# Two products interleaved from the first batch on, x of batch 0 by a casting DMA, and heads paired as neighbours

## The chip, the cores and the metric

One core of one Trainium2 chip. The metric is the device time of one execution in microseconds. A program's executions fall into a fast and a slow state; each run lists its granted TensorE clock. Profiles are of one execution, whose span is some 1.8 us shorter than its time.

## The reference, cut to what matters

```python
# x: (8, 8, 512, 64) batches, heads, rows, depth; state: (8, 8, 32, 64)
scores = scale * np.matmul(x, state.transpose(0, 1, 3, 2))   # softmax over the 32 states -> a
xread = np.matmul(a, state)
scores2 = scale * np.matmul(state, x.transpose(0, 1, 3, 2))  # softmax over the 512 rows -> a2
sread = np.matmul(a2, x)
attn = np.concatenate([xread, sread], axis=2)
# heads side by side: 4352 tokens of 512
h = tokens @ w_in                     # w_in 512 x 2048
out = gelu_exact(h) @ w_out           # w_out 2048 x 512
```

For each batch the kernel folds the state into the first weight (P = state times w_in, per head), so that the first product of a batch is P against the transposed attention weights a. The products: 256 matmuls of 128x512 for the first, 512 for the second, all batches together.

## The kernel before, cut to the parts concerned

Names as in the profile: `xb` is x of a batch as loaded (bf16), `x` the same rearranged by head pairs, `xT` its transpose, `pt` scores, `e` their exponentials, `a` normalised, `AT` its transpose, `p_ps`/`P` the folded weight, `hp`/`g` the first product and its Gelu, `op`/`osb` the second product and its eviction, `st_f`/`st_bf` states in fp32 and bf16. `pool` buffers with `space=PSUM` lie in the memory that TensorE writes to. Of the functions, `rearr` makes `x` of a batch, `xtr_dma` and `atr_dma` issue the transposing DMAs of `x` and of `a`, `scores`, `norm`, `pmat` and `sread` make `pt` and `e`, `a`, `P`, and the read of the state; a step of the first product is 2 matmuls and a Gelu (`M` in the changed kernel), a step of the second is 4 matmuls (`U`).

```python
ps_f = ctx.enter_context(tc.tile_pool(name="ps_f", bufs=6, space=bass.MemoryType.PSUM))
ps_o = ctx.enter_context(tc.tile_pool(name="ps_o", bufs=2, space=bass.MemoryType.PSUM))
...
st_rows = state.rearrange("b (t c) n d -> (c n) b t d", t=2)      # heads c and c+4 are a pair
nc.scalar.dma_start(out=st_f, in_=st_rows[:, 0, :, :])            # states of batch 0
...                                                               # x of batch 0: four fp32 DMAs, cast on VectorE
load_w_in(0)
load_w_in(1)
nc.gpsimd.dma_start(                                              # states of batches 1 to 7: ONE casting DMA
    out=st_bf[:, 1:B, :, :].rearrange("q b t d -> q (b t) d"),
    in_=st_rows[:, 1:B, :, :].rearrange("q b t d -> q (b t) d"),
)
load_x(1)
...
def steady(b):                       # what stands ahead of which first-product step of batch b
    nb = b + 1
    d[0] = [begin(nb), rearr(nb), load_x(b + 3), xtr_dma(nb)]     # lambdas left out
    d[4] = [scores(nb, 0), scores(nb, 1), norm(nb, 0), norm(nb, 1)]
    d[7] = [pmat(nb, (0, 1), act=((0, 1), (1, 1)))]
    d[8] = [atr_dma(nb)]
    d[12] = [sread(nb)]
    d[13] = [pmat(nb, (2, 3), act=((2, 1), (3, 1)))]
    d[14] = [srt(nb)]
...
lag = 16                             # the second product is 16 steps behind the first
mm1(b, s)                            # 2 matmuls and a Gelu
if done > lag:
    mm2(u)                           # 4 matmuls; two accumulators in turn
```

The softmax here doesn't subtract the row's maximum and nothing guards it: scores larger than these inputs give would overflow.

Of the kernel before, what the change touches and what calls it, by code (L numbers as in the profile page):

```python
# [17 lines left out]
def kernel(  # L18
# [25 lines left out]
    ps_f = ctx.enter_context(tc.tile_pool(name="ps_f", bufs=6, space=bass.MemoryType.PSUM))  # L44
    ps_o = ctx.enter_context(tc.tile_pool(name="ps_o", bufs=2, space=bass.MemoryType.PSUM))
# [11 lines left out]
    st_f = persist.tile([128, 2, D], FP32, name="st_f")  # L57
    st_bf = persist.tile([128, B, 2, D], BF16, name="st_bf")
    x0f = persist.tile([128, 2, HC, SJ * D], FP32, name="x0f")
    warm = persist.tile([128, 512], BF16, name="warm")  # L60
    ones = persist.tile([128, 1], BF16, name="ones")
# [3 lines left out]
    st_rows = state.rearrange("b (t c) n d -> (c n) b t d", t=2)  # L65
    x0_rows = x[0].rearrange("(t c) (p j) d -> p t c (j d)", t=2, j=SJ)
    nc.scalar.dma_start(out=st_f, in_=st_rows[:, 0, :, :])
    for c in range(HC):
        eng = nc.sync if c % 2 == 0 else nc.scalar
        eng.dma_start(out=x0f[:, :, c, :], in_=x0_rows[:, :, c, :])  # L70

    make_identity(nc, ident)
    nc.vector.memset(warm, 0.0)  # L73
    nc.gpsimd.memset(sbd, 0.0)
    nc.gpsimd.memset(ones, 1.0)

    def load_w_in(f):
        for t in range(2):
            nc.gpsimd.dma_start(  # L79
                out=w_in_bf[64 * t:64 * t + 64, :, f * 512:(f + 1) * 512],  # L80
                in_=moe_w_in[256 * t:256 * t + 256, f * 512:(f + 1) * 512].rearrange(
                    "(c d) f -> d c f", c=HC
                ),
            )
# [6 lines left out]
    xbs = {}  # L91

    def load_x(b):
        xb = xin.tile([128, H, SJ * D], BF16, name="xb", tag="xb")
        nc.gpsimd.dma_start(out=xb, in_=x[b].rearrange("h (p j) d -> p h (j d)", j=SJ))
        xbs[b] = xb

    load_w_in(0)
    load_w_in(1)
    nc.gpsimd.dma_start(  # L100
        out=st_bf[:, 1:B, :, :].rearrange("q b t d -> q (b t) d"),
        in_=st_rows[:, 1:B, :, :].rearrange("q b t d -> q (b t) d"),
    )
    load_x(1)
    load_w_in(2)
    load_w_in(3)
    load_w_out(0)
    load_w_out(1)
    load_x(2)
    load_w_out(2)  # L110
    load_w_out(3)
    load_x(3)


# [6 lines left out]
    def state_prep(b0, b1):  # L121
        n = b1 - b0
        if b0 == 0:
            nc.vector.tensor_copy(out=st_bf[:, 0, :, :], in_=st_f)
# [28 lines left out]
    def rearr(b):  # L153
        A = atts[b]
        eng = nc.vector if b < 3 else nc.gpsimd
        for t in range(2):
            eng.tensor_copy(  # L157
                out=A.x4[:, :, :, 64 * t:64 + 64 * t].rearrange("p j c d -> p c j d"),
                in_=xbs[b][:, 4 * t:4 * t + 4, :].rearrange("p c (j d) -> p c j d", d=D),
            )  # L160

    def rearr0(c):
        A = atts[0]
        nc.vector.tensor_copy(
            out=A.x4[:, :, c, :].rearrange("p j (t d) -> p t j d", t=2),
            in_=x0f[:, :, c, :].rearrange("p t (j d) -> p t j d", d=D),
        )

    def xtr0(c):
        A = atts[0]  # L170
        ps = ps_f.tile([128, SJ, 128], BF16, name="xT_ps", tag="f")
        for j in range(SJ):
            nc.tensor.transpose(ps[:, j, :], A.x4[:, j, c, :], ident)
        nc.scalar.copy(out=A.xT[:, :, c, :], in_=ps)

    def xtr(b, half):
        A = atts[b]
        ps = ps_f.tile([128, 2, SJ, 128], BF16, name="xT_ps", tag="f")
        for ci in range(2):
            for j in range(SJ):  # L180
                nc.tensor.transpose(ps[:, ci, j, :], A.x4[:, j, 2 * half + ci, :], ident)
        nc.vector.tensor_copy(out=A.xT[:, :, 2 * half:2 * half + 2, :].rearrange("p j c n -> p c j n"), in_=ps)

    def score_mms(b, c):
        A = atts[b]
        if c % 2 == 0:
            A.pt = ps_f.tile([128, SJ, 2, 2, NS], FP32, name="pt", tag="f")
        for j in range(SJ):
            nc.tensor.matmul(  # L189
                A.pt[:, j, :, c % 2, :],  # L190
                lhsT=A.xT[:, j, c, :],
                rhs=sbd[:, b, c, :],
                start=True,
                stop=True,
            )

    def expo(b, half):
        A = atts[b]
        nc.scalar.activation(  # L199
            out=A.e[:, :, 64 * half:64 * half + 64],  # L200
            in_=A.pt.rearrange("p j t c n -> p (j t) (c n)"),
            func=AF.Exp,
            scale=scale,
        )

    def xtr_dma(b):
        A = atts[b]
        nc.sync.dma_start_transpose(
            out=A.xT.rearrange("p j c n -> p (j c) n"), in_=A.x4.rearrange("p j c n -> p (j c n)")
        )  # L210

    def scores(b, half):
        score_mms(b, 2 * half)
        score_mms(b, 2 * half + 1)
        expo(b, half)
# [45 lines left out]
    def sread(b):  # L261
        A = atts[b]
        sr = ps_f.tile([128, 130], FP32, name="sr", tag="f")
        for o, n in ((0, D), (128, 1)):
            for t in range(2):
                for j in range(SJ):
                    for c in range(HC):
# [4 lines left out]
                            rhs=A.x4[:, j, c, 64 * t:64 * t + 64] if n == D else ones,  # L272
# [23 lines left out]
    def pmat(b, fs, act=()):  # L296
# [3 lines left out]
        for f in fs:  # L300
            ps = [ps_f.tile([128, 512], FP32, name="p_ps", tag="f") for t in range(2)]
# [10 lines left out]
        for f, ps in zip(fs, pss):  # L312
            for t in range(2):
                dst = Ps[b][:, t, f * 512:(f + 1) * 512]
                if (f, t) in act:
                    nc.scalar.copy(out=dst, in_=ps[t])  # L316
                else:
                    nc.vector.tensor_copy(out=dst, in_=ps[t])  # L318
# [33 lines left out]
    def mm2(u):  # L352
        b, r = u // 16, u % 16
        if b == 0:
            j, q = 2 * (r // 8) + r % 2, (r % 8) // 2
        else:
            j, q = r // 4, r % 4
        if q == 0:
            ops[j % 2] = ps_o.tile([128, d_model], FP32, name="op", tag="op")
        ps = ops[j % 2]  # L360
# [8 lines left out]
        if q == 3:  # L369
            rows = out[b * SB:b * SB + S, :].rearrange("(p j) n -> j p n", j=SJ)[j]  # L370
            evac(ps, [(rows, slice(0, 128))], last=(u == 16 * B - 1))
# [13 lines left out]
    def mm2_sr(s):  # L385
        ps = ps_o.tile([128, d_model], FP32, name="ops", tag="op")
# [14 lines left out]

    begin(0)
    keep_warm(6)
    state_prep(0, 1)
    for c in range(HC):
        rearr0(c)
    xtr0(0)
    xtr0(1)
    score_mms(0, 0)
    xtr0(2)  # L410
    score_mms(0, 1)
    expo(0, 0)
    xtr0(3)
    score_mms(0, 2)
    keep_warm(2)
    score_mms(0, 3)
    expo(0, 1)
    norm(0, 0)
    norm(0, 1)
    keep_warm(6)  # L420
    pmat(0, (0,), act=((0, 0), (0, 1)))
    keep_warm(4)
    atr(0)
    keep_warm(2)

    extra = {
        0: {
            1: [lambda: pmat(0, (1,))],
            3: [lambda: state_prep(1, B)],
            5: [lambda: begin(1), lambda: rearr(1), lambda: xtr(1, 0)],  # L430
            6: [lambda: xtr(1, 1), lambda: scores(1, 0), lambda: scores(1, 1)],
            7: [lambda: pmat(0, (2,))],
            8: [lambda: norm(1, 0), lambda: norm(1, 1)],
            10: [lambda: pmat(0, (3,))],
            12: [lambda: pmat(1, (0,))],
            13: [lambda: atr(1)],
            14: [lambda: pmat(1, (1,))],
        },
        1: {
            1: [lambda: sread(0), lambda: pmat(1, (2,))],  # L440
            2: [lambda: srt(0)],
            3: [lambda: pmat(1, (3,)), lambda: begin(2), lambda: rearr(2), lambda: xtr_dma(2)],
            4: [lambda: load_x(4), lambda: sread(1)],
            6: [lambda: srt(1)],
            8: [lambda: scores(2, 0), lambda: scores(2, 1), lambda: norm(2, 0), lambda: norm(2, 1)],
            10: [lambda: pmat(2, (0, 1), act=((0, 1), (1, 1)))],
            11: [lambda: atr_dma(2)],
            13: [lambda: sread(2)],
            14: [lambda: pmat(2, (2, 3), act=((2, 1), (3, 1)))],
            15: [lambda: srt(2)],  # L450
        },
    }

    def steady(b):
        nb = b + 1
        d = {}
        if nb >= B:
            return d
        d[0] = [lambda: begin(nb), lambda: rearr(nb)]
        if b + 3 < B:  # L460
            d[0].append(lambda: load_x(b + 3))
        d[0].append(lambda: xtr_dma(nb))
        d[4] = [
            lambda: scores(nb, 0),
            lambda: scores(nb, 1),
            lambda: norm(nb, 0),
            lambda: norm(nb, 1),
        ]
        d[7] = [lambda: pmat(nb, (0, 1), act=((0, 1), (1, 1)))]
        d[8] = [lambda: atr_dma(nb)]  # L470
        d[12] = [lambda: sread(nb)]
        d[13] = [lambda: pmat(nb, (2, 3), act=((2, 1), (3, 1)))]
        d[14] = [lambda: srt(nb)]
        return d

    u = 0
    lag = 16
    done = 0
    for b in range(B):
# [49 lines left out]
```

## Time and profile before

| | before |
|---|---|
| time, median of 3 | 236.54 us (236.05 to 237.08) |
| span of the profiled run | 234.7 us |
| TensorE busy | 217.1 us, 92% |
| granted clock | full from 12.2 us on |
| first matmul of the first product | 14.59 us |
| first matmul of the second product | 31.45 us |
| TensorE's largest wait | 5.4 us in six pieces, scores for the transposing DMA of x |

The views also show full clock before 12.2 us, but there the trace has no record of the clock: until then 128x512 matmuls last 0.61 to 0.63 us, and 0.38 us after, so the clock was at half.

Read the table from the last row up. TensorE sets the time; the waits and the start are all that a change of order can win.

### The profile page before, as it was taken

What the parts mean: (1) busy time and instruction counts of PE and PEld (TensorE: products, weight loads), DVE (VectorE), ACT (ScalarE), POOL (GpSimd) and SP (SyncE); (2) the same over time, 40 slices, a digit from 0 to 9 for tenths busy, and PEclk for the clock granted to TensorE, in tenths of its full rate; (3) what the DMA queues carried; (4) which work ended last, traced back from release to release, by engine and by line L of the source; (5) the groups of instructions that cost most, each with busy time, mean ns of one, the idle gap of its engine ahead of it and who ended that gap; (6) DMA issues with size and microseconds to landing.
All of it is one profiled execution on the core that took longest, in us unless ns stands there. A gap on an engine that the chain in (4) does not pass through costs nothing.

```text
span 234.7 us, 4315 instructions
## 1 busy us (share of the span) xinstructions
PE 217.1 (92%) x1844; PEld 100.7 (43%) x1844; DVE 85.3 (36%) x162; ACT 124.7 (53%) x208; POOL 28.1 (12%) x38
## 2 busy tenths in 40 slices
PE   5996799889979999999799999999999999999993
PEld 1543244434334444444344444444444444567441
DVE  2655974274135413631181317231623111111120
ACT  2577754485467446744494549454955454426000
POOL 8745001304000400030002000000000000000000
PEclk9999999999999999999999999999999999999999
DMA  7999999972923294252804061316131111211122
GB/s 205 149 178 206 202 205 185 126 161 26 226 76 86 56 165 98 62 75 53 128 0 106 31 143 38 89 47 134 46 92 45 47 45 55 80 46 47 27 65 87
DMA packets 38707, 23.12 MB, mean 98 GB/s; under 512 B 21920, under 2 KB 34464, under 8 KB 38688
## 3 DMA queue, kind: packets, MB, share of 16 engines
q0 software_dynamic: 13376, 8.09, 25.3%
q1 hardware_dynamic: 24352, 14.03, 24.8%
q10 hardware_dynamic: 960, 0.72, 1.0%
q8 instruction: 14, 0.23, 0.4%
q14 instruction: 5, 0.04, 0.1%
HBM read 17.30 MB, written 8.91 MB: 112 GB/s over the span
## 4 chain that ended last, share of the span: by engine, by line
PE 68%; DMA 18%; DVE 5%; ACT 3%; POOL 3%; issue 1%; SPq 1%; POOLq 0%; ACTq 0%
PE op L362 37%; PE hp L328 18%; DMA xT<-x 13%; DMA xb<-in_x_dram 5%; PE hps L376 3%; PE ops L388 3%; PE p_ps L304 3%; PE sr L269 2%; PE pt L189 2%; ACT g L335 2%; DVE osb L348 1%; POOL w_in_bf L79 1%; DVE P L318 1%; DVE a L226 1%; DVE cs L223 1%
## 5 line engine op out<-in xcount | busy, mean ns | idle before, releaser
L362 PE MATMUL op<-w_out_bf,g 128*128 128x512 bf16 x512 | 130.2, 379 | 0.0
L335 ACT ACTIVATE g<-hp 128x512 bf16<-128x512 f32 x128 | 74.5, 602 | 61.9 <-PE hp L328 61.7
L328 PE MATMUL hp<-AT,P 128*128 128x512 bf16 x256 | 75.9, 380 | 2.9 <-DVE P L318 1.5
L362 PEld LDWEIGHTS <-g 128*128 128x128 bf16 x512 | 50.1, 98 | 58.7
L348 DVE COPY osb<-op 128x512 f32<-128x512 f32 x31 | 21.4, 690 | 88.8 <-PE op L362 88.8
L328 PEld LDWEIGHTS <-P 128*128 128x128 bf16 x256 | 22.5, 98 | 30.2 <-issue 6.6
L318 DVE CAST P<-p_ps 128x512 bf16<-128x512 f32 x38 | 24.3, 684 | 11.1 <-PE p_ps L304 11.1
L157 POOL COPY x<-xb 128x1024 bf16<-128x1024 bf16 x10 | 10.1, 1044 | 93.3 <-PE sr L269 76.9
L316 ACT CAST P<-p_ps 128x512 bf16<-128x512 f32 x26 | 14.1, 601 | 6.1 <-PE p_ps L304 6.1
L223 DVE TENSOR_REDUCE cs<-e 128x16 f32<-128x512 bf16 x16 | 10.9, 682 | 17.2 <-ACT e L199 17.2
L199 ACT ACT_TABLE_LOAD x7 | 9.0, 1283 | 9.7 <-PE pt L189 9.7
L189 PE MATMUL pt<-sbd,xT 128*128 128x64 bf16 x128 | 6.3, 200 | 6.2 <-DMA xT<-x 5.4
L304 PE MATMUL p_ps<-w_in_bf,sbd 64*32 64x512 bf16 x256 | 11.9, 384 | 0.1
L226 DVE TENSOR_TENSOR a<-e,ics 128x512 bf16<-128x512 bf16 x16 | 11.1, 692 | 0.6
L383 ACT ACTIVATE g_sr<-hps 128x256 bf16<-128x256 f32 x16 | 6.1, 384 | 8.4 <-PE hps L376 8.0
L335 ACT ACT_TABLE_LOAD x8 | 10.3, 1283 | 0.1
L189 PEld LDWEIGHTS <-xT 128*128 128x128 bf16 x128 | 4.9, 102 | 10.5 <-DMA xT<-x 8.4
L199 ACT ACTIVATE e<-pt 128x512 bf16<-128x512 f32 x16 | 8.8, 595 | 0.7 <-PE pt L189 0.6
L118 PE MATMUL warm_ps<-warm 128*128 128x512 bf16 x20 | 7.9, 542 | 1.2 <-DVE warm L73 1.2
L376 PE MATMUL hps<-XSR,w_in_bf 128*128 128x256 bf16 x64 | 8.5, 273 | 0.0
L345 ACT COPY osb<-op 128x256 f32<-128x256 f32 x1 | 0.4, 372 | 13.9 <-DVE osb L343 13.9
L376 PEld LDWEIGHTS <-w_in_bf 128*128 128x128 bf16 x64 | 6.3, 98 | 2.7
(48 smaller groups left out, 81.8 us busy)
## 6 DMA issues: line engine op xcount, KB each, us to landing
out_dram<-osb SPq DMA_DIRECT2D x31, 256.0 KB, 2.3
xb<-in_x_dram POOLq DMA_DIRECT2D x7, 512.0 KB, 11.6
w_in_bf<-in_moe_w_in_dram POOLq DMA_DIRECT2D x8, 256.0 KB, 10.1
w_out_bf<-in_moe_w_out_dram POOLq DMA_DIRECT2D x4, 512.0 KB, 14.9
x0f<-in_x_dram SPq DMA_DIRECT2D x2, 256.0 KB, 3.4
x0f<-in_x_dram ACTq DMA_DIRECT2D x2, 256.0 KB, 4.3
out_dram<-osb SPq DMA_DIRECT2D x8, 64.0 KB, 1.7
st_bf<-in_state_dram POOLq DMA_DIRECT2D x1, 224.0 KB, 10.2
```

Of the source, the lines that this page charges most:

```text
L189: nc.tensor.matmul(A.pt[:, j, :, c % 2, :], lhsT=A.xT[:, j, c, :], rhs=sbd[:, b, c, :], start=True, stop=True,)
L199: nc.scalar.activation(out=A.e[:, :, 64 * half:64 * half + 64], in_=A.pt.rearrange("p j t c n -> p (j t) (c n)"), func=AF.Exp, scale=scale,)
L223: nc.vector.reduce_sum(out=cs, in_=e4, axis=AX.X)
L226: nc.vector.tensor_tensor(out=A.a[:, :, hs].rearrange("p g (c n) -> p g c n", n=NS), in0=e4, in1=ics[:, :, :].to_broadcast((128, G, 2, NS) ...
L304: nc.tensor.matmul(ps[t][32 * c:32 * c + 32, :], lhsT=sbd[64 * t:64 * t + 64, b, c, 32 * t:32 * t + 32], rhs=w_in_bf[64 * t:64 * t + 64, c ...
L316: nc.scalar.copy(out=dst, in_=ps[t])
L318: nc.vector.tensor_copy(out=dst, in_=ps[t])
L328: nc.tensor.matmul(hp, lhsT=Ps[b][:, t, m * 128:(m + 1) * 128], rhs=atts[b].AT[:, :, t, :], start=(t == 0), stop=(t == 1),)
L335: nc.scalar.activation(out=gs[b][:, m, :], in_=hp, func=AF.Gelu)
L348: nc.vector.tensor_copy(out=osb, in_=ps)
L362: nc.tensor.matmul(ps, lhsT=gs[b][:, m, j * 128:(j + 1) * 128], rhs=w_out_bf[:, m, :], start=(m == 0), stop=(m == MC - 1),)
L376: nc.tensor.matmul(hp, lhsT=w_in_bf[:, c, m * 128:(m + 1) * 128], rhs=XSR[:, c, :], start=(c == 0), stop=(c == HC - 1),)
```

## The change

The intent: start the second product after four steps instead of 16, and alternate pairs of first-product steps with pairs of second-product steps over four accumulators (so PSUM is split 4 and 4). Issue the transposing DMAs of x half a batch ahead. Load x of batch 0 with casting DMAs and transpose it as loaded. Pair heads h and h+1 so that a pair's 128 weight rows are contiguous.

```diff
-    ps_f = ctx.enter_context(tc.tile_pool(name="ps_f", bufs=6, space=bass.MemoryType.PSUM))
-    ps_o = ctx.enter_context(tc.tile_pool(name="ps_o", bufs=2, space=bass.MemoryType.PSUM))
+    ps_f = ctx.enter_context(tc.tile_pool(name="ps_f", bufs=4, space=PSUM))
+    ps_o = ctx.enter_context(tc.tile_pool(name="ps_o", bufs=4, space=PSUM))
...
-    st_rows = state.rearrange("b (t c) n d -> (c n) b t d", t=2)
+    st_rows = state.rearrange("b (c t) n d -> b t c n d", t=2)
...
-    nc.gpsimd.dma_start(
-        out=st_bf[:, 1:B, :, :].rearrange("q b t d -> q (b t) d"),
-        in_=st_rows[:, 1:B, :, :].rearrange("q b t d -> q (b t) d"),
-    )
+    def load_states():
+        for b in range(1, B):
+            for t in range(2):
+                nc.sync.dma_start(out=st_f[:, b, t, :], in_=st_rows[b, t])
...
+    norm0(0)
+    nc.vector.memset(st_f[0:1, 1, 0, 0:1], 0.0)      # holds the loads of the states back
+    load_states()
...
+    M(0, 1, 2, 3)                                     # first-product steps
+    U(0, 1)                                           # second-product steps
+    pmat(0, (1,), act=(1,))
+    U(2)
+    M(4)
+    U(3)
+    state_prep(1, B)                                  # needs the states of ALL later batches
...
+    U(15)
+    begin(2)
+    rearr(2)
+    xtr_dma(2)
...
+            if p == 2 and nb < B:
+                scores(nb, 0)
+                scores(nb, 1)
+                norm(nb, 0)
+                norm(nb, 1)
+            if p == 5 and nb < B:
+                atr_dma(nb)
+                ...
+                xtr_dma(nb + 1)
+            M(k, k + 1)
...
+            while u < k - 4:
+                U(u)
+                u += 1
+            if p == (2 if b == 1 else 1):
+                pmat(b, (2, 3), act=(1,))
```

## The prediction

> **What bounds the kernel now.** I read the page first (shares, slices, groups), then TensorE's list of waits, then the timeline of the start and of one whole batch.
>
> ```profile
> span 234.7 us, 4315 instructions
> PE 217.1 (92%) x1844; PEld 100.7 (43%) x1844; DVE 85.3 (36%) x162; ACT 124.7 (53%) x208; POOL 28.1 (12%) x38
> PE   5996799889979999999799999999999999999993
> ...
> L362 PE MATMUL op<-w_out_bf,g 128*128 128x512 bf16 x512 | 130.2, 379 | 0.0
> L335 ACT ACTIVATE g<-hp 128x512 bf16<-128x512 f32 x128 | 74.5, 602 | 61.9 <-PE hp L328 61.7
> L328 PE MATMUL hp<-AT,P 128*128 128x512 bf16 x256 | 75.9, 380 | 2.9 <-DVE P L318 1.5
> ```
>
> TensorE is the bound: 92% busy, and at 9 in nearly all slices after the first quarter. Its mean of 379 ns holds latency; the price is the distance between starts. Where the chain of waits lists second-product groups of four, each is 0.86 us long, so 0.216 us per 128x512 matmul. The two products then cost 768 x 0.216 = 165.9 us in either kernel. Only idle time and small work can change.
>
> TensorE's waits, "us in total, times, longest":
>
> ```profile
> PE pt L189 <- DMA xT<-x: 5.4, 6, 1.8
> PE hp L328 <- DVE P L318: 1.5, 4, 0.8
> PE hp L328 <- ACT g L335: 1.0, 1, 1.0
> ```
>
> The largest is the score matmul waiting for the transposing DMA of x, once in each of six batches. The timeline shows how that wait is made and what follows it on ScalarE (start, duration, engine, instruction):
>
> ```profile
> 133.94 0.69 DVE L348 COPY osb<-op 128x512 f32<-128x512 f32 x1 [2.37 <-PE op L362]
> 134.66 0.33 SPq L350 DMA_DIRECT2D out_dram<-osb  x1
> 135.09 2.17 SPq L208 DMA_TRANSPOSE xT<-x  x1
> ...
> 139.53 0.52 PEld L189 LDWEIGHTS <-xT 128*128 128x128 bf16 x16 [0.94 <-DMA xT<-x]
> 139.54 0.64 PE L189 MATMUL pt<-sbd,xT 128*128 128x64 bf16 x16 [0.45 <-DMA xT<-x]
> ...
> 140.01 1.28 ACT L199 ACT_TABLE_LOAD   x1 [1.16 <-PE pt L189]
> ...
> 141.31 1.09 ACT L199 ACTIVATE e<-pt 128x512 bf16<-128x512 f32 x2
> ...
> 142.41 1.28 ACT L335 ACT_TABLE_LOAD   x1
> ```
>
> SyncE issues in order: the eviction, the output's DMA, only then the transpose. The next first-product matmul began at 133.74, so the second product had stopped issuing then; scores could start at 139.54, 5.8 us later. The kernel before hides most of this under four steps of 1.3 us.
>
> The start:
>
> ```profile
> 14.59 0.76 PE L328 MATMUL hp<-AT,P 128*128 128x512 bf16 x2
> ...
> 18.50 0.76 DVE L157 COPY x<-xb 128x1024 bf16<-128x1024 bf16 x2 [0.16 <-DMA xb<-in_x_dram]
> ...
> 31.45 1.03 PE L362 MATMUL op<-w_out_bf,g 128*128 128x512 bf16 x4
> ```
>
> The first product starts at 14.59, the second only at 31.45 since it lags 16 steps. In these 17 us there is not work enough: 34 matmuls of the first product (7.3 us), five P groups (0.34 each), and transposes and scores (about 3) make some 12 us, leaving about 5 idle.
>
> **What the Trainium skill says.** "ScalarE: Activation LUTs", section "What ACT_TABLE_LOAD costs": about 1283 ns, plus about 1380 ns of drain. The load agrees (1283 ns in the groups). The drain is not seen: at 142.41 the load follows the second Exp, which ended at 142.40. I use 1.28. "PSUM — Partial Sum Buffer", section "PSUM: the matmul accumulator": eight banks of 2 KiB. The kernel before splits them 6 and 2, the new one 4 and 4, so four accumulators are paid for with two working buffers. "DMA: Bandwidth & Descriptors", section "SWDGE vs HWDGE vs iDMA": a casting DMA must be issued from GpSimd, and hardware generation is faster to set up. Before agrees: x0f landed 3.4 to 4.3 us after issue, while the queue of casts had its first packet at 5.33 for an issue at 3.04.
>
> **The change part by part.**
> *Start.* x of batch 0 now lands as bf16 from the software queue, issued at about 0.74 instead of behind memsets. First packet 2.3 us later (as above), 0.26 MB at the 0.2 MB/us of this queue's middle part, and 1.3 to 1.9 us from last packet to completion: the first half at about 5.9. It removes four casts on VectorE (2.06 us) but doubles the transposes to 64 rows, with 32 for 16 at 0.056 each in batches 0 and 1 (+0.9 each). From landing: 16 transposes 1.0, ScalarE copy 1.0, scores and two Exps, other half's copy on VectorE 0.7, last Exp and quarter-wise norm 2.4, eight transposes and copy 1.2: about 8.3 us. The first product starts at 14.2, a gain of 0.4. The early Gelu table load takes another 1.28 us off ScalarE there.
> *Second product from the first batch.* It starts after four steps instead of 16 and fills the 5 us hole. I walked the new order from 14.2 with row durations. It stalls about 0.5 at the first Gelu, 0.6 until the other states are in (14 small DMAs, issued late), 0.3 for a buffer, 0.8 where sread's division waits behind two norms, 0.7 elsewhere: 3 us against 5. Its last second-product group of batch 0 ends near 47.1, while there the pure work would end near 44.4. Weights arrive with about 3 us to spare in this order.
> *Scores of batch 2.* In the new order transpose(2) is issued after batch 0's last output, and scores(2) stand on TensorE directly after that group. Nothing hides the chain measured above: 5.8 us idle, in one place.
> *Batch 1 after it.* With four buffers, the P group behind scores(2) reuses the two score buffers and two first-product buffers. Score buffers are free at scores' start + 0.47 + 1.28 + 0.55 and 1.09 (140.01 and 141.31 rows); the other two after the Gelu table load and one or two Gelus at about 0.53 each. The first P group starts 1.5 us late and the second another 2.0: 3.5 us.
> *Steady batches.* Transposes are issued half a batch ahead: all six waits of the group disappear (5.4), also the 1.0 for ScalarE. But after scores the new order puts four first-product steps in a row; the third and fourth need the score buffers. At scores' start they are asked for 1.35 us later and free 2.35 and 2.87 later: about 1.15 us lost. In the batches preparing 3 and 4 the Exp table load has no wait of its own in the built program and can run early, so no loss; preparing 5, 6 and 7 it waits, as at 140.01: 3 x 1.15 = 3.5. P pairs go from 0.85 to 0.56 where their buffers are now free (six times, -1.7).
> *End.* Four outputs in a row instead of two pairs: +0.3 as an estimate.
>
> Sum on the span: start -0.4, early stalls -2, xT wait -5.4, ScalarE wait -1.0, P pairs -1.7, extra transposes of batch 1 +0.9, more changes of work in the first batches +0.8, scores(2) +5.8, batch 1 +3.5, steady +3.5, end +0.3 = +4.3. A direct sum from 47.1 gives 5.8 + 3.5 + 3.5 stalls, 171.4 of remaining issue work, 2.8 of changes (0.43 per batch), 4.5 tail: 238.6, so +3.9. The span is 1.8 below the timed median. I put the time at 240.0.
>
> **The rivals.**
> First: the two stalls of batch 1 do not happen, because TensorE is late there anyway or the transpose lands quickly. Then the 9.3 go and the time is about 231, just over 2% faster. For it: the design aims at that, and ScalarE has 47% idle. Against: SyncE's order is fixed, and the six landings of this transpose in before took 4.4 to 6.1 us.
> Second: the start is bound by the queue of casts. x of batch 0 now stands before all weights; the four weight chunks and x(1) need 3 MB before the second quarter of the first product. If it moves 0.15 rather than 0.2 MB/us, as it did near 12 us, stalls grow by 3 to 5 us and the time goes to 244. For it: DMA is at 9 of 10 in eight slices. Against: my walk found some 3 us of slack.
> Third: pairing itself makes TensorE faster by fewer alternations. In before a step of six matmuls takes 1.297 us, exactly six times 0.216; nothing is to be won, and the time stays at 240.
>
> **Range and chances.** The errors are the early walk (2 us either way), the three steady stalls (0 to 3.5), the stall at scores(2) (5 to 7.5). Together about 3 us: 236.0 to 243.5 eight times in ten. The 2% limits are 231.8 and 241.3. Faster needs the first rival (6%); slower needs only 1.3 us more than my sum (32%); the rest, 62%, within 2%.
>
> **What will show it.** Right: one TensorE idle stretch of 5 to 7 us near 47 to 53 ended by the transposing DMA; no other wait on it; waits of p_ps for ScalarE after it; three waits of hp for Exp near 1 us in later batches; the second product's first group near 16.5. Wrong: no idle of that size there, or idle spread before 45 us on weights' DMAs.

## The result, and the profile after

The changed kernel took 268.04 us (266.90 to 268.62, 4 runs) against 236.81 for before (236.05 to 240.78, 4 runs: the three of the table above and a slow one): 13.25% slower, interval 12.7 to 13.8%. Ratios here and below are the mean time of one kernel's fast runs over that of before's fast runs of the same rounds, so they are not quite the ratio of the medians.

The head and the slices of its page (40 slices, each digit tenths; PEclk is the granted clock):

```profile
span 266.8 us, 4389 instructions
PE 220.7 (83%) x1867; PEld 101.8 (38%) x1867; DVE 81.5 (31%) x160; ACT 121.3 (45%) x214; POOL 28.7 (11%) x38
...
PE   4794000998918999999999989998998999999992
PEclk9999555699985899999999999999999999999999
```

Busy time of TensorE hardly changed (217.1 to 220.7); what is new is idle time. Three slices of zero near 27 to 47 us, one of 1 near 75 us, and under both a clock of half. The second half of the span looks as good as before, or better.

TensorE's waits (us in total, times, longest):

```profile
PE st_ps L126 <- DVE st_bf L123: 24.3, 1, 24.3
PE pt L220 <- DMA xT<-x: 5.7, 1, 5.7
PE hp L346 <- ACT e L227: 2.7, 3, 0.9
PE xT_ps L169 <- DMA xb<-in_x_dram: 2.4, 1, 2.4
PE p_ps L322 <- ACT g L353: 1.3, 1, 1.3
```

The first line is 24.3 us of a loss of 31, and the prediction gave it 0.6 us. The next, third and fifth are the stalls that it did name. The first stall in the timeline (SPq is SyncE's queue, its duration that of all its issues together):

```profile
11.62 26.43 SPq L103 DMA_DIRECT2D st_f<-in_state_dram  x14
...
21.95 1.03 PE L376 MATMUL op<-w_out_bf,g 128*128 128x512 bf16 x4
...
46.60 0.63 DVE L123 CAST st_bf<-st_f 128x896 bf16<-128x896 f32 x1 [25.14 <-DMA st_f<-in_state_dram]
47.28 0.93 PE L126 MATMUL st_ps<-ident,st_bf 128*128 128x128 bf16 x7 [24.30 <-DVE st_bf L123]
```

The 14 loads of states, 32 KB each and 448 KB in all, were being issued for 26 us, and the last had landed only at 46.5. VectorE's cast waits for all of them, TensorE for the cast. One line of the view of that tile says how long an issue took:

```profile
L103 SPq DMA_DIRECT2D st_f<-in_state_dram x14: 529/1442/6210, 11.6 to 35.9; - x14
```

Shortest, median, longest in ns: 0.5 us is the bare issue, up to 6.2 us is waiting. Eight semaphores take turns for SyncE's DMAs, so the ninth load uses that of the first. But this is not what held it up: the first load had landed at 16.2, and the ninth began to issue at 18.17 and was done only at 24.4, when the fifth landed (24.44). The issues of the tenth, eleventh and twelfth likewise end within 0.5 us of the landing of the load four places ahead. These loads land one after the other, 3.2 to 3.4 us apart (24.44, 27.79, 31.14, 34.48, 37.69), with others always issued behind them: what takes the time is moving the data. The completions of the semaphore of the first and of the ninth load, in us from the start of the span, taken from the trace's semaphore updates:

```
first load, issued 11.62:  12.6 (at issue)   15.3 15.4 16.2 16.2
ninth load, issued 18.17:  24.8 (at issue)   36.0 36.1 36.4 37.7
```

Four completions for each, where an output's DMA in the same trace has sixteen. The Trainium skill, page "DMA: Bandwidth & Descriptors", section "Why a DMA increments its semaphore by 16 and not by 1", says why: a DMA issued by hardware is spread over the largest number of engines, up to 16, that divides the slowest dimension of both access patterns, the missing completions are written at once, and the rest come as each engine's data land. The source here is `c n d` with c = 4, so 4 of 16. The trace agrees: five updates, one at issue and four later.

The second stall, as the prediction drew it from the kernel before:

```profile
73.72 0.69 DVE L366 COPY osb<-op 128x512 f32<-128x512 f32 x1 [1.04 <-PE op L376]
74.88 2.14 SPq L178 DMA_TRANSPOSE xT<-x  x1
79.42 0.88 PEld L220 LDWEIGHTS <-xT 128*128 128x128 bf16 x16 [6.23 <-DMA xT<-x]
```

### The profile page after: what moved, and what is told of

Its sections match the earlier page's. It is cut to its first block, busy times and chain, and to the rows that moved or that the text cites. A ratio compares the mean times of both kernels' runs of the same rounds, so it can differ in the third digit from the quotient of the medians.

```text
span 266.8 us, 4389 instructions
## 1 busy us (share of the span) xinstructions
PE 220.7 (83%) x1867; PEld 101.8 (38%) x1867; DVE 81.5 (31%) x160; ACT 121.3 (45%) x214; POOL 28.7 (11%) x38
## 4 chain that ended last, share of the span: by engine, by line
PE 70%; SPq 9%; DMA 8%; ACT 5%; DVE 4%; issue 2%; DVEq 0%; ACTq 0%; POOLq 0%
PE op L376 38%; PE hp L346 18%; SPq L103 9%; DMA st_f<-in_state_dram 4%; PE p_ps L322 3%; PE hps L390 3%; PE ops L402 3%; DMA xb<-in_x_dram 2%; ACT L227 2%; DMA xT<-x 2%; PE sr L286 2%; PE xT_ps L169 1%; ACT e L227 1%; ACT g L353 1%; DVE a L243 1%
## 5 line engine op out<-in xcount | busy, mean ns | idle before, releaser
L376 PE MATMUL op<-w_out_bf,g 128*128 128x512 bf16 x512 | 123.8, 383 | 0.3
L353 ACT ACTIVATE g<-hp 128x512 bf16<-128x512 f32 x128 | 67.9, 601 | 84.5 <-PE hp L346 84.4
L346 PE MATMUL hp<-AT,P 128*128 128x512 bf16 x256 | 66.7, 388 | 3.1 <-ACT e L227 2.7
L336 DVE CAST P<-p_ps 128x512 bf16<-128x512 f32 x32 | 20.7, 684 | 39.2 <-PE p_ps L322 39.1
L366 DVE COPY osb<-op 128x512 f32<-128x512 f32 x31 | 20.8, 687 | 36.6 <-PE op L376 36.6
L334 ACT CAST P<-p_ps 128x512 bf16<-128x512 f32 x32 | 17.5, 588 | 24.0 <-PE p_ps L322 14.9
L156 POOL COPY x<-xb 128x1024 bf16<-128x1024 bf16 x12 | 12.6, 1083 | 129.7 <-PE sr L286 129.7
L126 PE MATMUL st_ps<-ident,st_bf 128*128 128x128 bf16 x8 | 1.2, 308 | 24.3 <-DVE st_bf L123 24.3
L240 DVE TENSOR_REDUCE cs<-e 128x16 f32<-128x512 bf16 x14 | 9.5, 681 | 12.9 <-ACT e L227 12.9
L220 PE MATMUL pt<-sbd,xT 128*128 128x64 bf16 x112 | 4.8, 200 | 5.7 <-DMA xT<-x 5.7
L366 DVE COPY osb<-ops 128x512 f32<-128x512 f32 x2 | 1.4, 692 | 26.3 <-PE ops L402 26.3
L295 DVE RECIPROCAL inv<-sr 128x2 f32<-128x2 f32 x8 | 1.4, 169 | 21.9 <-PE sr L286 21.9
## 6 DMA issues: line engine op xcount, KB each, us to landing
w_in_bf<-in_moe_w_in_dram POOLq DMA_DIRECT2D x4, 512.0 KB, 11.6
```

The lines of the kernel that those rows point to most:

```text
L156: eng.tensor_copy(out=A.x4[:, :, :, 64 * t:64 * t + 64].rearrange("p j c d -> p c j d"), in_=xbs[b].rearrange("p (c t) (j d) -> p t c j d" ...
L334: nc.scalar.copy(out=dst, in_=ps[t])
L336: nc.vector.tensor_copy(out=dst, in_=ps[t])
L346: nc.tensor.matmul(hp, lhsT=Ps[b][:, t, m * 128:(m + 1) * 128], rhs=atts[b].AT[:, :, t, :], start=(t == 0), stop=(t == 1),)
L353: nc.scalar.activation(out=gs[b][:, m, :], in_=hp, func=AF.Gelu)
L366: nc.vector.tensor_copy(out=osb, in_=ps)
```

## The experiments

Before was run on the same chip beside each group of runs. Its medians there were 237.72 (e1 to e4), 239.08 (e5 to e8) and 237.68 (e9 to e11), and in the second and third group more than half of its executions were slow; so ratios are given, not only times. All eleven kernels gave correct results.

### e1: the same states over 16 engines

```diff
-        for b in range(1, B):
+        for c in range(HC):
             for t in range(2):
-                nc.sync.dma_start(out=st_f[:, b, t, :], in_=st_rows[b, t])
+                nc.sync.dma_start(
+                    out=st_f[NS * c:NS * c + NS, 1:B, t, :],
+                    in_=state[1:B, 2 * c + t, :, :].rearrange("b n d -> n b d"),
+                )
```

> The changed kernel, with the states of batches 1 to 7 loaded at the same place and on the same queue, same bytes and same 256-byte packets, but in 8 DMAs whose slowest dimension is 32 rows on both sides instead of 14 whose source's slowest dimension is 4. Theory K (each of the 14 DMAs runs on 4 of the 16 DMA engines, as its completions arriving four at a time suggest): the states land near 20 to 25 us instead of 46.5, TensorE's wait for st_bf falls from 24.3 to under 4 us, the granted clock after it stays at full, time 238 to 245. Theory L (the states are late because they are issued at 11.6 us, after the gate, behind the queue of casts): the wait stays above 15 us and the time above 258.

Measured: 243.61 us, ratio 1.0311 (1.0195 to 1.0427). The states had landed at 20.9 us instead of 46.5. The tile's line and two of TensorE's waits:

```profile
L103 SPq DMA_DIRECT2D st_f<-in_state_dram x8: 367/446/606, 10.4 to 13.9; - x8
```

```profile
PE pt L223 <- DMA xT<-x: 8.7, 1, 8.7
...
PE st_ps L129 <- DVE st_bf L126: 0.3, 1, 0.3
```

Same bytes, same 256-byte packets, same queue, same place in the program (the issue starts at 10.4 instead of 11.6): the number of engines changed, and with it the number of loads, 8 instead of 14. The wait went from 24.3 to 0.3 us. Theory K stands. No run varies the number of loads alone, but the landings 3.2 to 3.4 us apart above, 32 KB each, are against it as the cause: here a load of 56 KB lands 5.1 to 6.9 us after its issue with up to seven others in flight. Sixteen completions follow each load. The remaining clock at half (49.4 to 63.1 us) contradicts the expectation that the clock would stay full: it now follows the second stall. That stall is longer than in the changed kernel (8.7 us): the transpose took 7.5 us from issue to landing, against 4.5 there. The likely reason, argued and not tested, is that the kernel arrives there earlier, with a casting load still in flight (x of a later batch landed at 51.8).

### e2: the 14 loads at the start, without the gate

```diff
     begin(0)
+    load_states()
...
-    nc.vector.memset(st_f[0:1, 1, 0, 0:1], 0.0)
-    load_states()
```

> The changed kernel with its 14 state DMAs unchanged but issued at the start of the queue, without the gate that holds them until 11.5 us. Theory K: 14 DMAs on 4 engines at 2 to 3 us each still need 28 to 42 us, so they land near 32 to 40, the wait stays at 8 to 18 us, time 250 to 262. Theory L: they land before 20 us, the wait disappears, time 238 to 243.

Measured: 265.13 us, ratio 1.1224 (1.1086 to 1.1362).

```profile
PE st_ps L126 <- DVE st_bf L123: 20.8, 1, 20.8
```

Ten microseconds earlier in issue bought three in time. Lateness (theory L) is refuted as the cause. My figure for K was too low as well: I took 2 to 3 us for each load, and the last landed at 42.8, not 32 to 40, and wait and time were above the ranges that I gave for K. The reason shows in the landings of the casting DMAs, which share those four engines: x of batches 2 and 3 landed at 43.5 and 46.2 here, 41.7 and 46.0 in the changed kernel, and 36.2 and 38.8 in e1. In the changed kernel twelve of the sixteen completions of x of batch 2 came by 36.6, the other four from 40.5 to 41.7. Both kinds of load slow each other.

### e3: filling matmuls in the first stall

```diff
     U(3)
+    wps = ps_f.tile([128, 512], FP32, name="warm_ps", tag="f")
+    for _ in range(112):
+        nc.tensor.matmul(wps, lhsT=warm[:, 0:128], rhs=warm, start=True, stop=True)
     state_prep(1, B)
```

> The changed kernel with 112 idle-filling matmuls (24.2 us of TensorE) put in front of the transposes that wait for the states; nothing else. If the low granted clock (0.5 from 27.3 to 51.2 us) costs only what runs slowly after the wait, the clock stays at full there and the time falls by 1 to 3 us, to 265 to 267; the later low stretch from 78.5 to 88.7 stays. If the filling delays the work behind it, the time rises by up to 2.

Measured: 266.65 us, ratio 1.1302 (1.1207 to 1.1397) against 1.1325: some 1.4 us less in the medians, but the intervals overlap. The traces are clearer. The clock was full from 15.2 to 76.6 us, and the stretch from the states' transposes to the scores of batch 1 took 3.55 us (46.65 to 50.20), against 5.26 (47.28 to 52.54) in the changed kernel, where the clock is at half until 51.2. So the first low stretch of 23.9 us cost 1.7 of the 31 us: for most of it TensorE had nothing to do. The later low stretch stayed only in part (76.6 to 80.0 and 83.4 to 86.8).

### e4: e1 and an earlier transpose of x of batch 2

```diff
     atr(1)
+    begin(2)
+    rearr(2)
+    xtr_dma(2)
     U(10)
...
     U(15)
-    begin(2)
-    rearr(2)
-    xtr_dma(2)
```

> As e1, and in addition the rearrangement and the transposing DMA of batch 2 are issued before the outputs of batch 0, some 9 us earlier. My theory of the second part of the loss: the 5.7 us wait of the scores of batch 2 disappears and with it the half clock that follows it (about 4 us more), so 8 to 11 us less than e1: 228 to 236. Rival: the transpose is held up elsewhere (x of batch 2 lands late, the rearrangement is late), then within 3 us of e1.

Measured: 236.83 us, ratio 1.0029 (0.9925 to 1.0133), 6.8 us under e1 and just outside my range.

```profile
PE p_ps L325 <- ACT g L356: 1.5, 1, 1.5
PE pt L223 <- DMA xT<-x: 1.5, 1, 1.5
```

The wait for the transpose fell from 8.7 to 1.5. It did not vanish since x of batch 2 now is the limit: it lands at 37.1, GpSimd rearranges it, the transpose is issued at 39.27 and takes 8.2 us to 47.50, beside the last casting loads. The clock was again at half, from 51.7 to 58.5, in the stretch behind the scores of batch 2, where P waits for its buffers.

### e5: e4 and P before the scores in batch 1

```diff
+            if p == 2 and b == 1:
+                pmat(b, (2, 3), act=(1,))
+                U(u, u + 1)
+                u += 2
             if p == 2 and nb < B:
                 scores(nb, 0)
...
-            if p == (2 if b == 1 else 1):
+            if p == 1:
                 pmat(b, (2, 3), act=(1,))
```

> As e4 (states on 16 engines, early transpose for batch 2), and in batch 1 the P group of column chunks 2 and 3 with two second-product steps stands before the scores of batch 2 instead of behind them. Theory (four working buffers: the P group waits for the score buffers and the two first-product buffers, 3.5 us by my prediction, 2.5 us in e4's list of waits, and half clock follows): the waits of p_ps for ScalarE go, the half clock near 52 to 58 us too, time 229 to 233 against 236.8 for e4. Rival (the wait only moves to the transposing DMA or to the next first-product steps): within 1.5 us of e4.

Measured: 234.30 us, ratio 0.9906 (0.9745 to 1.0067). Just above the range, and the interval overlaps that of e4, so a gain over e4 is not shown by the times.

```profile
PE hp L349 <- ACT e L230: 4.7, 5, 1.0
```

The waits of p_ps for ScalarE are gone from the list and so is the half clock after 14 us, but the first product now waits five times for Exp instead of three (2.7 us in e4): batch 1 has taken over the pattern of the later batches. The rival's half is true: part of the wait only moved.

### e6: e4 and the scores behind a pair of first-product steps

```diff
-            if p == 2 and nb < B:
-                scores(nb, 0)
-                scores(nb, 1)
-                norm(nb, 0)
-                norm(nb, 1)
...
             M(k, k + 1)
+            if p == 3 and nb < B:
+                scores(nb, 0)
+                scores(nb, 1)
+                norm(nb, 0)
+                norm(nb, 1)
```

> As e4, and in every batch the scores of the next batch stand after the first-product pair of step 3, in front of two second-product steps, so that no first-product step asks for a score buffer sooner than 2.6 us after. Theory: the three waits of hp for Exp (2.7 us) and those of batch 1 (2.5 and 1.5 us) all go, with the half clock near 52 to 58: 225 to 230. Rival (ScalarE is then late with Gelu, and op waits for g): 231 to 236.

Measured: 227.43 us (227.00 to 228.37), ratio 0.9613 (0.9445 to 0.9781). TensorE's slices and the largest waits left after 14 us:

```profile
PE hp L349 <- ACT g L356: 0.7, 1, 0.7
PE hp L349 <- ACT AT L265: 0.5, 1, 0.5
```

```profile
PE   5689999998999999999999999999999999999991
```

No wait for Exp, for a P buffer or for a transpose is left. The buffers of the scores are now asked for after two second-product steps (1.7 us) and the next first-product steps do not queue behind them. This version beats before by about 4% in this group (2.8% in e11) and the changed kernel by 15%.

### e7: e6 with more filling at the start

The edit adds three calls of `keep_warm` (6, 2 and 2 matmuls) among the first transposes.

> As e6 with ten more filling matmuls in the first 10 us (six before the transposes of x, two after each half). In e4's profile the clock was at half from 7.3 to 14.1 us, in e1's it was not. If fillers hold the clock: 0.5 to 2 us faster than e6, and less scatter; if they are in the way of the chain of the start: up to 1 us slower.

Measured: 228.13 us, ratio 0.9626 (0.9506 to 0.9746): no difference from e6 that the intervals show. The fillers did what they should: the clock was full from 4.2 us on, where e6's 128x512 matmuls last 0.61 to 0.63 us until 13.96, so at half clock (and e1's until 15.3, which the expectation read as full, since the trace has no record there). The first product started at 12.97 instead of 14.22. But TensorE then waited 2.7 us for the states instead of 0.3, and the states' transposes began at 22.66 instead of 21.43: on 16 engines too, the states set the pace of the start there. The same text as e6 shows a 2.0 us wait there in e11.

### e8: the kernel before with early transposes only

```diff
-        d[0] = [lambda: begin(nb), lambda: rearr(nb)]
+        d[0] = []
         if b + 3 < B:
             d[0].append(lambda: load_x(b + 3))
-        d[0].append(lambda: xtr_dma(nb))
...
         d[8] = [lambda: atr_dma(nb)]
+        if nb + 1 < B:
+            d[8] += [lambda: begin(nb + 1), lambda: rearr(nb + 1), lambda: xtr_dma(nb + 1)]
```

> The kernel before with one idea of the change alone: rearrangement and transposing DMA of x half a batch ahead (behind the transposing DMA of a, from batch 3 on). Theory: the waits of pt for xT in batches 2 to 6 go (4.0 of 5.4 us), 232 to 234. Rival (hidden anyway by something that ends later): within 1 us of before.

Measured: 232.47 us, ratio 0.979 (0.955 to 1.003). The median is where theory put it, but the interval includes no change, and the profile fell in the slow state, so its lines are not used for sizes. It lists one wait of the scores for the transpose in place of six, that of batch 2. I call the gain likely, not shown.

### e9: heads paired in halves again

The edit puts back the loading layout of before for state, weights and x, and nothing of the order. Its core:

```diff
-    st_rows = state.rearrange("b (c t) n d -> b t c n d", t=2)
+    st_rows = state.rearrange("b (t c) n d -> (c n) b t d", t=2)
...
-        for b in range(1, B):
-            for t in range(2):
-                nc.sync.dma_start(out=st_f[:, b, t, :], in_=st_rows[b, t])
+        nc.sync.dma_start(
+            out=st_f[:, 1:B, :, :].rearrange("q b t d -> q (b t) d"),
+            in_=st_rows[:, 1:B, :, :].rearrange("q b t d -> q (b t) d"),
+        )
```

> The changed kernel with one part of the change undone: heads paired as h and h+4 again, as in the kernel before, so the states of batches 1 to 7 are one DMA of 128 partitions at the same place and on the same queue (and the weights' first chunks and x of batch 0 need twice as many casting DMAs). Theory K: the pairing of neighbours is what split the states into 14 DMAs on 4 engines; with it undone the wait for st_bf is under 4 us and the time within 3 us of e1, 240 to 247, of which about 1 us for the more numerous DMAs of the start. Rival (another part of the change makes the states late): wait above 10 us, time above 252.

Measured: 244.35 us, ratio 1.0419 (1.0313 to 1.0525).

```profile
PE pt L225 <- DMA xT<-x: 8.8, 1, 8.8
PE hp L351 <- ACT e L232: 2.7, 3, 0.9
PE st_ps L131 <- DVE st_bf L128: 1.4, 1, 1.4
```

With that one part undone, the wait for the states is 1.4 us and the time is near that of e1. The one DMA landed at 24.1, 13.7 us after its issue. The pairing of neighbours, with its loads written as they were, is the part of the change that carried the loss (e1 keeps the pairing and writes them otherwise): with pairs h and h+4 the 128 rows of a state tile form one dimension of the source, with neighbours they are 4 groups of 32.

### e10: e1 with filling matmuls in the second stall

```diff
+    wps = ps_f.tile([128, 512], FP32, name="warm_ps", tag="f")
+    for _ in range(40):
+        nc.tensor.matmul(wps, lhsT=warm[:, 0:128], rhs=warm, start=True, stop=True)
     for b in range(1, B):
```

> As e1, with 40 filling matmuls (8.6 us of TensorE) where it waits 8.7 us for the transposing DMA of batch 2. e1's granted clock is 0.5 from 49.4 to 63.1 us. If the low clock after a wait costs work, the clock stays full and the time falls by 2.5 to 5 us from e1's 243.6, with the wait itself filled, not shortened: 238.5 to 241. Rival (TensorE in that stretch is bound by ScalarE and VectorE anyway): within 1 us of e1.

Measured: 245.10 us in the median, fast runs 243.45 to 245.94, ratio 1.0405 (1.0294 to 1.0516) against e1's 1.0311: no gain. The profile (clock 0.95) is an indication only. The stretch from the scores of batch 2 to the first-product steps of step 3, of e1:

```profile
54.27 1.04 PE L223 MATMUL pt<-sbd,xT 128*128 128x64 bf16 x16 [8.74 <-DMA xT<-x]
...
63.46 0.81 PE L349 MATMUL hp<-AT,P 128*128 128x512 bf16 x3
```

and of e10:

```profile
56.25 0.63 PE L223 MATMUL pt<-sbd,xT 128*128 128x64 bf16 x16
...
65.22 1.97 PE L349 MATMUL hp<-AT,P 128*128 128x512 bf16 x8
```

9.19 us at half clock in e1. In e10, 8.97 us, the clock was at 0.95 until 61.4 and then at half until 64.8. This does not prove the rival, for two reasons. The transpose had landed at 53.88, so the filling, which ended near 56.3, held the scores up for some 2.4 us in this profile. And the clock fell again just where TensorE had work. Profiles of fast runs separate the two. The part from the scores to the second P group, where the waits for ScalarE lie, took 5.11 us at half clock in e1 (54.27 to 59.38) and 4.90 in e4 (47.55 to 52.45), where the clock was full until 51.7. The part from there to the first-product steps took 4.08 us at half clock in e1 and 2.57 in e9 (62.63 to 65.20), where it was full from 61.3. So half clock cost some 0.2 us while TensorE waited, and 1.5 us in the dense work behind. In the changed kernel the same stretch took 9.43 us (79.42 to 88.85), at half clock too.

### e11: e6 again, five rounds

The text is that of e6.

> The same text as e6, again in five rounds, for an interval: 226.5 to 229, 3 to 5% faster than before.

Measured: 228.74 us (227.38 to 229.12), ratio 0.9724 (0.9673 to 0.9774) against before's fast runs alone, of which there were four among eleven. The interval leaves out no gain; the time is in the range and the gain just under the 3 to 5% that I expected: 2.8% here, 3.9% in e6's group, whose before ran slower. Its own times agree with e6 within 1.3 us.

## Why the prediction was wrong, point by point

The forecast was 240.0 us with 236.0 to 243.5; it was 268.0. The step that failed is the term of the early walk that reads "0.6 until the other states are in (14 small DMAs, issued late)". It measured 24.3 us. I saw that they were small and late, and took their landing from DMAs that run on all 16 engines. I did not look at the shape of the source, though the rule for the number of engines stands on a page of the skill that I had cited for another section. e1 and e9 show that this term is nearly the whole miss: with the states on 16 engines the kernel took 243.6 and 244.4, just above the upper end of the range.

The second rival came near in kind (a start bound by DMA; it gave 244 us) but named the wrong queue. The casting queue carried 0.17 to 0.19 MB/us from 16 to 36 us, near the 0.2 that I took; weights were never the wait in the changed kernel. The first rival failed: both stalls of batch 1 came. The third failed as forecast: in steady work twelve matmuls took 2.60 us (139.64 to 142.24), 0.216 each as before.

The other terms, against the changed kernel or e1:

- Scores of batch 2 on the transposing DMA: 5.8 predicted, 5.7 measured. The form of this stall was read off the kernel before in three lines, but the size agrees by luck: the stall of the states had moved it to 74 us, where the transpose took 4.5 us. Near 47 us, where I had placed it, it measured 8.7 in e1, with a transpose of 7.5 us.
- Batch 1 after it: 3.5 predicted. From the end of the scores to the second-product steps took 5.31 us in the changed kernel (80.27 to 85.58), where two pairs of first-product matmuls and the P group need about 1.5 at full clock (0.87, 0.56 and 0.1): 3.8. The clock was at half there.
- Three steady stalls of 1.15 each, only where the Exp table load has a wait of its own: three waits were measured, 2.7 us in the list. First-product matmuls occupy 8.05 us instead of 6.92 in each of those batches, so 1.13 each.
- Transposes half a batch ahead: five of the six waits went, and the one of batch 2 stayed, as forecast.
- Start: 14.2 predicted, 15.42 measured; 14.2 in e1. The first half of x landed at 6.45 in the one and 5.24 in the other; e1's edit does not touch it, so this is scatter between runs.
- End of batch 0's second product, without the states' stall: 47.1 predicted, 45.4 in e1, from the starts of matmuls. My early walk was 1.7 too long, and the transpose's longer wait in e1 more than made up for it.
- The clock: not in the prediction at all. "TensorE: Matmul & The Clock Gate" of the skill, section "What's actually happening", has the clock fall to half after an idle window of 3.4 us. The trace agrees: half from 27.3 to 51.2 us and from 78.5 to 88.7, which is 7 and 3 windows of 3.41. As far as the traces show, it cost 1.7 us in the first stretch (e3) and some 2 us in the second: behind the scores of batch 2 the part that waits took 5.11 us against 4.90 at nearly full clock in e4, the dense part 4.32 against 2.57 at full clock in e9.

From the states' transposes to the end the changed kernel and e1 need the same 219.5 us (47.28 to 266.8 and 21.63 to 241.3, within 0.2). So the difference of 25.5 us between them lies ahead of that point: 24.0 in the wait and 1.2 in the start. That the rest is equal is a balance: e1 waits 3.0 us longer for the transpose, and the changed kernel loses 1.7 at half clock before the scores of batch 1 and about 1.2 elsewhere.

Two slips in the text change nothing: DMA is at 9 in nine slices, not eight, and the two sums, with the 1.8 us between span and time, give 240.8 and 240.4, not 240.0.

What is left open: whether 14 loads on 16 engines would do as well as 8 (no run varies the number alone), and how much of e6's gain over before belongs to the early second product and how much to the early transposes. e8 says about 2% for the latter, with an interval that includes zero.

## What to carry to other kernels

When a change of layout splits a load into several DMAs, look at the slowest dimension of each access pattern, not only at bytes and packet sizes: 4 instead of 32 or 128 there cost 24 us for 448 KB. A load that everything later waits for should be checked for the number of its completions in the trace. And when an instruction stands in an engine's order directly behind what another queue has to finish first, add up that queue's chain: it showed here where TensorE would stall, though the size, 5.7 or 8.7 us, depended on what else the DMA engines were doing.

## What the Trainium skill lacked or had wrong

- "DMA: Bandwidth & Descriptors" has the rule for the number of engines, but no cost for breaking it. Here 14 DMAs of 32 KB on 4 engines took from 11.6 to 46.5 us beside a busy casting queue, and the same bytes on 16 engines from 10.4 to 20.9 (e1, 8 DMAs) and to 24.1 (e9, one DMA). The casting queue suffered too: its last initial load landed at 46.0 instead of 38.8.
- The same page, "Latency and other measured facts", gives about 1 us to the first byte of a software DMA. The first packet came 2.3 us after the start of its issue in before (3.04 to 5.33) and 1.6 us in the changed kernel (1.24 to 2.84), of which the issuing instruction itself lasted 0.9.
- "ScalarE: Activation LUTs", "What ACT_TABLE_LOAD costs", adds about 1380 ns of drain to each table load. No such time shows: the load at 142.41 begins 0.01 us after the activation before it and takes 1.28, and the next activation starts at 143.71, 0.02 after its end.
- "TensorE: Matmul & The Clock Gate" does not separate low clock while TensorE waits from low clock while it has work. Here 23.9 us at half clock cost 1.7, and in the second stall the part that waits for ScalarE took 5.11 us at half clock (e1) and 4.90 at nearly full clock (e4), the dense part behind it 4.08 at half clock (e1) and 2.57 at full clock (e9).
